# Values' loads on ACT's DMA queue, keys' on SP's: a windowed attention decode step with a gated branch

## Chip, cores and metric

One core of one Trainium2 chip. The metric is the device time of one execution in microseconds; several executions are run and the median is given. The time before is 216.89 us (median of 3 runs, 216.76 to 216.92).

## What is computed

Two tokens (batch 2, one new position each) go through an attention over the last 4096 positions of a cache of 32768, and through a small gated branch; the attention's output is scaled by the branch's. Cut to what matters:

```
W = 4096                                   # window: the last W of Sk = 32768 positions
xn = layernorm(x)                          # x: 2 x 1 x 512
q  = (xn @ wq) as 32 heads of 128          # wq: 512 x 4096
k  = k_cache[:, :, Sk-W:, :]               # 2 x 8 x W x 128, each kv head serves 4 query heads
v  = v_cache[:, :, Sk-W:, :]
p  = softmax(q k^T * 128**-0.5)
s  = (p v, heads joined) @ wo              # wo: 4096 x 512
z  = gelu(xn @ w_in)                       # w_in: 512 x 1792
g  = silu(z1 * (w_sp * layernorm(z2) + b_sp) @ w_out)
out = x + s * g
```

All is float32. The windows of keys and values are 33.6 MB each, wq and wo 8.4 MB each, w_in and w_out 5.5 MB together: every byte is read once and used for one or two vectors.

## The kernel before

The 16 pairs of batch and kv head are taken two at a time: eight *units* (`NU`), each with one tile of keys (`k0` to `k7`) and one of values (`v0` to `v7`). Such a tile is 128 partitions x 32 KB, 4 MB, and is loaded by one DMA (`load`, L146). Keys, values, w_in, wq and wo all share one ring of four buffers of that size (`ring`, L105; `slot`, L111). A load can be issued only when the tile that used its buffer four allocations earlier is no longer read. In order of allocation the ring holds win, wq0, wq2, k0, k1, v0, k2, v1, k3, v2, k4, v3, k5, v4, k6, v5, k7, v6, v7, wo0, wo1. So from k3 on a key tile waits for the key tile two units earlier to have been turned (its last step is T:u.7), and from v2 on a value tile for the value tile two units earlier to have been multiplied (pv:u.1); v7, wo0 and wo1 wait for T:6.7, pv:5.1 and T:7.7.

Every DMA of the bulk is issued by SP, in the order in which the program names it. ACT issues four small loads at the start (x twice, w_sp, b_sp). The order of the steps on every engine is written out by hand in `ORDER` (L27 to L52): a word like `T:3.5` is step T of unit 3, part 5. The words are walked from first to last (L607 to L611), `step` (L572) calls the function, and `InOrder` (L55) makes each engine keep that order. [...]

The steps of a unit, with engine and names in the profile:

- `T` (`turn`, L377, DVE): eight transposes in blocks that turn the keys, `kts<-k`. Two buffers hold half a unit each.
- `shares` (L387, PE, `sh<-kts,qb`), `keep` (L397, ACT, `ss<-sh`), `scores` (L401, PE, `s<-ss,sums`): the scores of one half.
- `rowmax`, `mg`, `shmax`, `bias` (DVE, PE): the maximum and the bias `nb`; `exp` (L430, ACT, `p<-s,nb`); `probs_t` (L438, DVE, `pT<-p`).
- `pv` (L455, PE, `acc<-v,pT`): the values, half a unit each; `lsum`, `shsum`, `weights` (DVE, PE): the sums' reciprocals.
- `evac` (L466, ACT, `o<-acc,wd`), `col`, `gather`, `spread`, `oT`: the unit's output, brought into the layout of the product with wo.
- `X`, `Y`, `U` (`wo_early`, L530, PE, `part<-wo,oT`) and `Z` (`wo_last`, L548, PE, `so<-wo,oT`): the product with wo, block by block as its six DMAs land (`load_wo`, L518).

Steps of two units are interleaved: pv:u.0 stands behind T:(u+1).6 and scores:(u+1).0 behind pv:u.0, so that PE multiplies unit u's values while DVE turns unit u+1's keys. In `ORDER` the words `K:u+1 V:u` stand together at the start of a line, behind evac:u-2 of the line before (V:0 and V:1 behind nothing of that kind), and V:7 stands before wo:0. The hand-written order of unit 2's line, as an example:

```
K:3 V:2 T:2.0 T:2.1 T:2.2 rowmax:1.1 mg:1 shmax:1 T:2.3 bias:1 shares:2.0 T:2.4 exp:1.0 probs_t:1.0 T:2.5 T:2.6 exp:1.1
keep:2.0 pv:1.0 lsum:1 shsum:1 scores:2.0 T:2.7 shares:2.1 probs_t:1.1 pv:1.1 weights:1 keep:2.1 scores:2.1 evac:1
```

In the profile nearly all instructions have line L65, the helper's, so groups are told apart by their tiles.

Of the kernel before, what the change touches and what calls it, by code (L numbers as in the profile page):

```python
# [70 lines left out]
def kernel(  # L71
# [14 lines left out]
    pe, dve, act, sp = (InOrder(tc, e) for e in (nc.tensor, nc.vector, nc.scalar, nc.sync))  # L86
# [24 lines left out]
    def slot(name, *shape):  # L111
        return ring.tile([P, *shape], F32, tag="slot", name=name)
# [14 lines left out]
    for a in range(0, KT, 2):  # L127
        t = slot(f"wq{a}", 2, HQ * DH)
# [14 lines left out]
    NU = NP // 2  # L143
    UJ = 2 * NT

    def load(u, src, name):  # L146
        t = slot(f"{name}{u}", UJ, DH)
        b, v = divmod(u, HKV // 2)
        first = src[b, 2 * v, SK - W, :]
        of = bass.AP(tensor=src.tensor, offset=first.offset, ap=[[UJ * DH, P // 2], [SK * DH, 2], [1, UJ * DH]])  # L150
        sp.dma_start(t.rearrange("p j d -> p (j d)"), of)
        return t


# [120 lines left out]
    u = cst.tile([P, 2, FT, B], F32, tag="u", name="u")  # L275
# [65 lines left out]
    def place_queries():  # L341
        dve.tensor_tensor(
            free_ap(qb, 16, [[REP, G], [32, NP * G], [1, REP]]), free_ap(qa, 0, [[0, G], [REP, NP * G], [1, REP]]),
            free_ap(grpm, 0, [[1, G], [0, NP * G], [0, REP]]), op=ALU.mult,
        )
# [3 lines left out]
    def silu():  # L349
        dve.tensor_scalar(gate, ys, -1.0, 80.0, op0=ALU.mult, op1=ALU.min)  # L350
        act.activation(gate, gate, AF.Exp)
        dve.tensor_scalar_add(gate, gate, 1.0)
        dve.reciprocal(gate, gate)
        dve.tensor_mul(gate, gate, ys)
# [139 lines left out]
    def spread(i):  # L494
        o1, oT, nj = sets[f"oT{i}"]
        pts[i] = bank(f"oT_ps{i}", B, 32)
        pe.matmul(pts[i], perms[nj][0].rearrange("p h a x -> p (h a x)"), o1, start=True, stop=True)

    def place(i):
        _, oT, nj = sets[f"oT{i}"]  # L500
        nx = 32 // nj
        t = sb.tile([P, B, nx, nj], F32, tag="ot", name=f"ot{i}", bufs=1)
        dve.tensor_tensor(
            t, pts[i].rearrange("p b (x j) -> p b x j", x=nx), free_ap(perms[nj][1], 0, [[0, B], [1, nx], [0, nj]]),
            op=ALU.mult,
        )
        dve.tensor_reduce(
            oT[:, :, 0 : 16 * B : 16].rearrange("p j b -> p b j"), t.rearrange("p b x j -> p b j x"), axis=AX.X, op=ALU.add
        )
# [8 lines left out]
    def load_wo(n):  # L518
        t = slot(f"wo{n}", 16, D)
        a = 0  # L520
        for i in ((0,), (1, 2))[n]:
            for j, n in (((0, 16),), ((0, 8),), ((0, 4), (4, 2), (6, 1), (7, 1)))[i]:
                sp.dma_start(t[:, a : a + n, :], wo_s[i][:, j : j + n, :])
                blocks.append((t[:, a : a + n, :], sets[f"oT{i}"][1], j))
                a += n
# [4 lines left out]
    def wo_early(n, at):  # L530
        nonlocal done
        if done == 0:
            part.append(ps.tile([P, 512], F32, tag="s0", name="part"))
        t, oT, j = blocks[n]
        for a in range(at, at + 2):
            g = done % G
            pe.matmul(
                part[0][32 * g : 32 * g + 32, :], oT[:, j + a, :], t[:, a, :], start=(done < G), stop=(done >= EARLY - G)
            )
            done += 1  # L540
# [3 lines left out]
    def copy_parts():  # L544
        parts.append(sb.tile([P, D], F32, tag="o", name="parts", bufs=1))
        act.activation(parts[0], part[0], AF.Copy)

    def wo_last(n):  # L548
        if n == 0:
            so.append(bank("so", DC))  # L550
        t, oT, j = blocks[3 + n]
        for a in range(t.shape[1]):
            for g in range(G):
                pe.matmul(
                    so[0][32 * g : 32 * g + 32, :], oT[:, j + a, :], t[:, a, g * DC : (g + 1) * DC],
                    start=(n == 0 and a == 0), stop=(j + a == oT.shape[1] - 1),
                )

    def add_parts():
        for g in range(G):  # L560
            pe.matmul(
                so[0][32 * g : 32 * g + 32, :], rowm, parts[0][:, g * DC : (g + 1) * DC], start=False, stop=False
            )
# [8 lines left out]
    def step(name, u, a=()):  # L572
        if name == "q":
            place_queries()
        elif name == "silu":
            silu()
        elif name == "K":
            units[u].k = load(u, k_cache, "k")
        elif name == "V":
            units[u].v = load(u, v_cache, "v")  # L580
        elif name == "wo":
            load_wo(u)
        elif name == "spread":
            spread(u)
        elif name == "oT":
            place(u)
        elif name == "X":
            wo_early(0, 2 * a[0])
        elif name == "Y":
            wo_early(1, 2 * a[0])  # L590
        elif name == "U":
            wo_early(2, 2 * a[0])
        elif name == "Z":
            wo_last(u)
        elif name == "parts":
            copy_parts()
        elif name == "pz":
            add_parts()
        else:
            STEPS[name](units[u], *a)  # L600

    units = []
    for u in range(NU):
        p = Unit()
        p.u, p.m, p.kt, p.sh, p.ss, p.s, p.p, p.pT = u, None, {}, {}, {}, {}, {}, {}
        units.append(p)
    for line in ORDER.strip().split("\n"):  # L607
        for name in line.split():
            name, at = name.split(":")
            u, _, a = at.partition(".")  # L610
            step(name, int(u), (int(a),) if a else ())  # L611
# [33 lines left out]
```

## Time and profile before

| | before |
|---|---|
| median of the runs | 216.89 us (216.76 to 216.92) |
| the profiled execution | 217.29 us, span 215.5 us |
| mean granted TensorE clock | 0.825 |
| busy: PE / DVE / ACT / POOL | 143.2 / 126.7 / 51.6 / 4.5 us |
| read from HBM | 89.40 MB, 415 GB/s over the span |
| keys, issue to landing (median of 8) | 27.4 us |
| values, issue to landing (median of 8) | 29.8 us |
| DVE waiting for keys, in total | 29.5 us, 7 times |
| PE waiting for values, in total | 4.3 us, 5 times |

The span runs from the first to the last instruction of the program; the time has some 1.8 us more around it. "Busy" leaves out instructions that only issue a DMA or wait for a semaphore. A DMA queue is named by its number: q1 carries what SP issues, q10 what ACT issues; both are served by the same 16 DMA engines, and q8 and q14 fetch instructions. `SPq` and `ACTq` are the two engines' instruction streams, where a DMA's issue appears with the time that issuing took, not the time of the transfer. Behind "<-" in square brackets stands what ended the idle time before an instruction.

### The profile page before, as it was taken

To read this page: it belongs to the slowest core of one execution; us is meant where nothing else is said; L and a number is where in the kernel's file an instruction comes from. 1 tells how busy PE (TensorE), PEld (TensorE's weight loads), DVE (VectorE), ACT (ScalarE), POOL (GpSimd) and SP (SyncE) were. 2 spreads that over 40 slices of the span, in tenths; PEclk is the share of its full clock that TensorE was granted. 3 is DMA by queue.
4 is the path that set the end of the run, shared out by engine and by line. 5 is a ranking of instruction groups with operands and counts; after the bars stand their busy time and mean duration, and the time that the engine had idled before them with its cause. 6 is when DMAs were issued, how large, how long until landed. Compare 5 with 4: busy or idle time off the path is not lost.

```text
span 215.5 us, 2332 instructions
## 1 busy us (share of the span) xinstructions
PE 143.2 (66%) x900; PEld 48.1 (22%) x900; DVE 126.7 (59%) x218; ACT 51.6 (24%) x129; POOL 4.5 (2%) x17
## 2 busy tenths in 40 slices
PE   0179796833854966964991795389259917987793
PEld 0117622111120221222220231123112201232231
DVE  2611213169899799649928972993698099636011
ACT  5011103300116036033330602142051206142201
POOL 8000000000000000000000000000000000000000
PEclk9999569665998896796697599669755997996999
DMA  7999999999999999999999999999999999999990
GB/s 246 432 443 444 398 429 465 414 458 414 456 408 447 420 426 444 426 443 426 450 420 450 408 441 420 426 450 426 447 415 456 401 456 414 447 426 417 420 374 22
DMA packets 3930, 89.54 MB, mean 416 GB/s; under 512 B 446, under 2 KB 462, under 8 KB 848
## 3 DMA queue, kind: packets, MB, share of 16 engines
q1 hardware_dynamic: 3900, 89.40, 96.8%
q8 instruction: 7, 0.11, 0.2%
q14 instruction: 3, 0.02, 0.0%
q10 hardware_dynamic: 20, 0.01, 0.0%
HBM read 89.40 MB, written 0.00 MB: 415 GB/s over the span
## 4 chain that ended last, share of the span: by engine, by line
DMA 63%; PE 23%; DVE 8%; ACT 3%; issue 1%; ACTq 0%
DMA v<-in_A_v_cache_dram 42%; DMA k<-in_A_k_cache_dram 16%; PE acc L65 10%; DMA win<-in_B_w_in_dram 5%; PE sh L65 5%; DVE kts L65 4%; PE part L65 4%; PE s L65 3%; DVE pT L65 1%; ACT p L65 1%; ACT o L65 1%; DVE gate L65 1%; PE mo L65 1%; ACT ss L65 1%; DVE qb L65 1%
## 5 line engine op out<-in xcount | busy, mean ns | idle before, releaser
L65 DVE STREAM_TRANSPOSE kts<-k 128x1024 f32<-128x1024 f32 x64 | 75.6, 1218 | 29.5 <-DMA k<-in_A_k_cache_dram 29.5
L65 PE MATMUL sh<-kts,qb 128*32 128x512 f32 x256 | 41.6, 775 | 13.2 <-DVE kts L65 9.3
L65 PE MATMUL acc<-v,pT 128*32 128x512 f32 x256 | 37.4, 707 | 8.8 <-DVE pT L65 4.4
L65 ACT ACTIVATE p<-s,nb 128x512 f32<-128x512 f32 x32 | 22.5, 733 | 36.2 <-DVE nb L65 36.2
L65 ACT ACTIVATE ss<-sh 128x512 f32<-128x512 f32 x16 | 9.6, 599 | 59.1 <-PE sh L65 59.1
L65 DVE STREAM_TRANSPOSE pT<-p 128x1024 f32<-128x1024 f32 x16 | 19.6, 1225 | 2.3 <-ACT p L65 2.1
L65 PE MATMUL s<-ss,sums 128*128 128x512 f32 x32 | 18.8, 671 | 2.3 <-ACT ss L65 2.3
L65 PE MATMUL mo<-mg,joint 128*128 128x16 f32 x16 | 4.0, 327 | 23.4 <-DVE mg L65 23.4
L65 PEld LDWEIGHTS acc<-v,pT 128*32 128x32 f32 x256 | 10.5, 145 | 35.1 <-issue 27.0
L65 PEld LDWEIGHTS sh<-kts,qb 128*32 128x32 f32 x256 | 8.8, 126 | 34.2 <-issue 28.8
L65 DVE TENSOR_REDUCE m<-s 128x1 f32<-128x512 f32 x16 | 10.7, 671 | 4.2 <-PE s L65 4.2
L65 PE MATMUL q_ps<-wq,xnT 128*32 128x512 f32 x64 | 10.5, 784 | 3.5 <-DMA wq<-in_A_wq_dram 3.5
L65 ACT ACTIVATE o<-acc,wd 128x128 f32<-128x128 f32 x32 | 9.1, 368 | 15.0 <-PE acc L65 15.0
L65 PEld LDWEIGHTS mo<-mg,joint 128*128 128x128 f32 x16 | 3.2, 250 | 27.2 <-DVE mg L65 24.4
L65 PE MATMUL z<-win,xnT 128*32 128x448 f32 x32 | 5.6, 869 | 4.7 <-DMA win<-in_B_w_in_dram 4.7
L65 PE MATMUL part<-wo,oT 128*32 128x512 f32 x56 | 7.7, 596 | 1.4 <-ACT o L65 1.4
L65 PEld LDWEIGHTS s<-ss,sums 128*128 128x128 f32 x32 | 5.0, 197 | 10.3 <-issue 7.7
L65 PE MATMUL zT_ps<-rowm,z 128*128 128x2 f32 x28 | 6.6, 370 | 0.0
L65 PEld LDWEIGHTS zT_ps<-rowm,z 128*128 128x128 f32 x28 | 6.5, 325 | 0.0
L65 ACT ACTIVATION_READ_ACCUMULATOR p<-s,nb 128x1 f32 x32 | 6.5, 203 | 0.0
L65 ACT ACT_TABLE_LOAD x4 | 5.1, 1283 | 2.6 <-POOL hT L164 2.6
L65 DVE COPY z<-z 128x448 f32<-128x448 f32 x2 | 1.3, 626 | 7.5 <-PE z L65 7.5
(111 smaller groups left out, 68.4 us busy)
## 6 DMA issues: line engine op xcount, KB each, us to landing
k<-in_A_k_cache_dram SPq DMA_DIRECT2D x8, 4096.0 KB, 27.4
v<-in_A_v_cache_dram SPq DMA_DIRECT2D x8, 4096.0 KB, 29.8
wq<-in_A_wq_dram SPq DMA_DIRECT2D x1, 4096.0 KB, 24.5
wq<-in_A_wq_dram SPq DMA_DIRECT2D x2, 2048.0 KB
wo<-in_A_wo_dram SPq DMA_DIRECT2D x1, 4096.0 KB, 30.4
win<-in_B_w_in_dram SPq DMA_DIRECT2D x1, 3584.0 KB, 11.5
wo<-in_A_wo_dram SPq DMA_DIRECT2D x1, 2048.0 KB
wout<-in_B_w_out_dram SPq DMA_DIRECT2D x1, 1792.0 KB, 15.3
```

The costliest lines, as they stand in the source:

```text
L65: return self.tc.keep_in_program_order(call(*args, **kwargs))
```

## The change

`load` is given the engine that issues the DMA. Keys are issued by SP as before, values by ACT, except the last unit's, which SP issues as before. The words of `ORDER`, the ring, the tiles and all computation are the same.

```diff
-    def load(u, src, name):
+    def load(u, src, name, queue):
         t = slot(f"{name}{u}", UJ, DH)
         b, v = divmod(u, HKV // 2)
         first = src[b, 2 * v, SK - W, :]
         of = bass.AP(tensor=src.tensor, offset=first.offset, ap=[[UJ * DH, P // 2], [SK * DH, 2], [1, UJ * DH]])
-        sp.dma_start(t.rearrange("p j d -> p (j d)"), of)
+        queue.dma_start(t.rearrange("p j d -> p (j d)"), of)
         return t
...
         elif name == "K":
-            units[u].k = load(u, k_cache, "k")
+            units[u].k = load(u, k_cache, "k", sp)
         elif name == "V":
-            units[u].v = load(u, v_cache, "v")
+            units[u].v = load(u, v_cache, "v", act if u < NU - 1 else sp)
```

In the built program seven DMA issues leave SP's stream. In ACT's stream v0 stands behind `ys`, v1 behind keep:0.1, and v2 to v6 behind evac:0 to evac:4. The streams of PE, DVE and POOL are the same instruction for instruction.

## The prediction

> **What bounds the kernel now.** I read the page first for the share of the DMA engines, then a table by stretches for where they are full, then the chain that ended last for what the end waits on, then the timelines of the queues and engines that the edit touches.
>
> ```profile
> span 215.5 us, 2332 instructions
> ...
> q1 hardware_dynamic: 3900, 89.40, 96.8%
> ```
>
> The profiled execution took 217.29 us, 1.8 more than its span and 0.4 above the median of the runs (216.89). All 89.40 MB of real loads go through one queue, q1 (SP's), and keep the 16 DMA engines busy for 96.8% of the span. By stretches (PE, PEld, DVE, ACT and POOL busy, then PE clock, DMA share, GB/s):
>
> ```profile
> 52.00:102.00 50.00, 35.32 (x206) 10.20 (x210) 41.02 (x55) 13.15 (x36) 0.00 (x0) 0.84 1.00 429
> ...
> 152.00:202.00 50.00, 33.66 (x200) 10.27 (x200) 32.37 (x51) 14.33 (x40) 0.00 (x0) 0.80 1.00 430
> 202.00:210.00 8.00, 7.49 (x66) 2.86 (x66) 0.78 (x3) 0.01 (x1) 0.00 (x0) 1.00 0.95 395
> ```
>
> The DMA share is 1.00 from 52 to 202 and drops only with the last bytes (0.95 from 202 to 210). So the loads are the floor, no compute engine is (DVE, the busiest, has 41.0 of 50), and a change of queue cannot shorten what is already gapless. It can change the order in which 4 MB transfers land. The end does depend on that order. From the chain in order of time (start, length, what):
>
> ```profile
> 77.09 27.29 DMA v<-in_A_v_cache_dram
> ...
> 150.21 32.33 DMA v<-in_A_v_cache_dram
> ```
>
> These are units 2 and 6: v2 lands at 77.09 + 27.29 = 104.38, v6 at 150.21 + 32.33 = 182.54. Between them land k4 v3 k5 v4 k6 v5 k7 v6, eight transfers in 78.16 us, so one 4 MB transfer takes 9.77 us. Counting back 13 transfers from v6, k1 landed at about 55.5. From v6 on, the end is a chain of computation (PE):
>
> ```profile
> 182.68 1.95 PE L65 MATMUL acc<-v,pT 128*32 128x512 f32 x16 [1.12 <-DMA v<-in_A_v_cache_dram]
> ...
> 185.62 1.97 PE L65 MATMUL sh<-kts,qb 128*32 128x512 f32 x16
> ...
> 198.80 1.95 PE L65 MATMUL acc<-v,pT 128*32 128x512 f32 x16
> 202.11 2.34 PE L65 MATMUL part<-wo,oT 128*32 128x512 f32 x18 [1.36 <-ACT o L65]
> ```
>
> These rows are pv:6.0, shares:7.1, pv:7.1, then the first of the early wo products X. Between pv:7.1's end (200.75) and the first X (202.11) lie 1.36 us. The row names ACT's o, which these matmuls don't read. wo's first transfer is two behind v6, 182.54 + 2 x 9.77 = 202.08, and that is what X waited for. So this tail has two nearly equal gates: the wo loads, which the edit doesn't make later, and the chain from pv:6.0, with 1.36 us of slack.
>
> **The change part by part.** Nothing in work or bytes is removed or added. Seven DMA issues leave SP's instruction stream and stand in ACT's, each where V:u stands in the written order; PE, DVE and POOL keep their instructions.
>
> *SP without them.* Keys were issued when DVE had freed their buffer; no values' issue ahead of them held them up:
>
> ```profile
> 32.50 0.53 SPq L65 DMA_DIRECT2D v<-in_A_v_cache_dram  x1
> 39.53 0.54 SPq L65 DMA_DIRECT2D k<-in_A_k_cache_dram  x1
> 56.46 0.54 SPq L65 DMA_DIRECT2D v<-in_A_v_cache_dram  x1
> 71.88 0.54 SPq L65 DMA_DIRECT2D k<-in_A_k_cache_dram  x1
> 77.09 0.54 SPq L65 DMA_DIRECT2D v<-in_A_v_cache_dram  x1
> ```
>
> Each issue takes 0.54 us and the queue sits for 5 to 17 us between them, so SP saves 7 x 0.54 us that nobody waited for: nothing gained.
>
> *ACT with them.* The neighbours in ACT's order:
>
> ```profile
> 46.04 0.28 ACT L65 ACTIVATE ys<-y_sum 128x128 f32<-128x128 f32 x1 [3.37 <-PE y_sum L65]
> 55.34 0.60 ACT L65 ACTIVATE ss<-sh 128x512 f32<-128x512 f32 x1 [9.01 <-PE sh L65]
> 59.24 0.60 ACT L65 ACTIVATE ss<-sh 128x512 f32<-128x512 f32 x1 [3.31 <-PE sh L65]
> 63.39 0.31 ACT L65 ACTIVATE gate<-gate 128x128 f32<-128x128 f32 x1 [3.55 <-DVE gate L65]
> ...
> 77.09 1.14 ACT L65 ACTIVATE o<-acc,wd 128x128 f32<-128x128 f32 x4 [1.06 <-PE acc L65]
> 81.21 0.74 ACT L65 ACTIVATE p<-s,nb 128x512 f32<-128x512 f32 x1 [2.98 <-DVE nb L65]
> ```
>
> v0 follows ys, v1 the second ss (keep:0.1), and v2 to v6 the o of evac:0 to evac:4. The buffer of each is already free there (evac:u needs the same pv:u.1 that frees v:u), so ACT does not wait at the issue; 0.54 us falls into idle times of 9.01, 3.55 and 2.98; exp of the later units waits for nb in the same way. Cost on ACT: none, covered by that wait; with that cover gone it would be 0.54 us per unit ahead of exp. The issues come later, though: v1 at 59.84 instead of 56.46, v2 at 78.23 instead of 77.09 (evac's 1.14). Those two stand behind some 28 us of queue and cost nothing. v0 moves most, from 32.50 to 46.32, and that puts k2 (39.53) ahead of it in time.
>
> *Two queues instead of one.* This is the term that counts. The trace has one stretch in which ACT's queue (q10) holds packets while SP's has win, wout and wq outstanding. ACT's small loads are issued at
>
> ```profile
> 0.74 0.55 ACTq L65 DMA_DIRECT2D xs<-in_A_x_dram  x1
> 1.33 0.24 ACTq L65 DMA_DIRECT2D wb<-in_B_w_sp_dram  x1
> 1.59 0.27 ACTq L65 DMA_DIRECT2D wb<-in_B_b_sp_dram  x1
> 1.90 0.63 ACTq L65 DMA_DIRECT2D x<-in_A_x_dram  x1
> ```
>
> and the DMA queues show, from 2 to 5.8 us (first row) and from 5.8 to 11.4 (the two after it), packets, MB and share:
>
> ```profile
> q1 hardware_dynamic: 39, 1.12, 70.6%
> ...
> q1 hardware_dynamic: 103, 2.37, 98.0%
> q10 hardware_dynamic: 16, 0.00, 0.3%
> ```
>
> After xs, no packet of q10 passes for four microseconds from the last issue (1.90 to 5.8); then 16 pass while q1 is 98.0% busy. q1's bytes of the two stretches, 3.49 MB, are fewer than win's 3.67 (128 x 7168 floats), so those 16 passed inside the first bulk load, with wout and wq queued behind it. So a second queue is neither put behind all of the first's bytes nor served at once: it waits for some packets already taken in, and then both are served in turns. For 32 KB packets on both sides I take turns as half the rate each.
>
> [...]
>
> Let s be the time of v0's first packet. After s, seven values' transfers go at half rate beside keys, so v6 lands 14 transfer times later: s + 14 x 9.77 = s + 136.8. Lower bound of s: xs, on empty queues, was issued at 0.74 and read by DVE at 2.15,
>
> ```profile
> 2.15 0.68 DVE L65 BATCH_NORM_STATS2 st<-xs 2x6 f32<-2x512 f32 x1
> ```
>
> 1.4 us, so 46.32 + 1.4 = 47.7. Upper: behind all that was queued on SP, k1's end, 55.5 (q10's last packets waited 9.5 us: 55.8). I take a wait of 5 us, nearest to the first q10 packets (5.8 minus 1.33 is 4.5, and the packets are a little larger here): s = 51.3. Then v6 lands at 188.1, 5.6 late. pv:6.0 moves by that, everything behind it on PE too, and the 1.36 of slack ahead of X is used up first: **+4.2 us**.
>
> The keys pay for what the values gain. k1 has 55.5 - s left at s and needs twice that; k2 to k7 follow at 2 x 9.77 each; so k7 lands 55.5 - s late (4.2 at s = 51.3). DVE then turns it:
>
> ```profile
> 172.91 1.25 DVE L65 STREAM_TRANSPOSE kts<-k 128x1024 f32<-128x1024 f32 x1 [6.66 <-DMA k<-in_A_k_cache_dram]
> ...
> 181.86 2.33 DVE L65 STREAM_TRANSPOSE kts<-k 128x1024 f32<-128x1024 f32 x2
> ```
>
> The last turn ended at 184.19 and shares:7.1 began at 185.62: 1.43 of slack. So shares:7.1 is late by 54.1 - s through k7 and by s - 45.7 through v6, whichever is more. The least of the two together is 4.2 (s = 49.9), which leaves +2.8 at the end: no s makes it free. At s = 47.7 it is 6.4 through k7, +5.0. At s = 55.5 it would be 9.8 through v6, +8.4; but k3 is issued at 71.88, only some 3 us before k2 lands (55.5 + 2 x 9.77 = 75.0), so with such waits SP's queue runs dry at each unit and the values catch up; I cap this end at +6.5. Everything after X keeps its lengths. wo0's issue waits for pv:5.1 and slips by as much, but v7 is in flight ahead of it until 182.54 + 9.77 = 192.3, so wo lands as before. In the middle the same lateness makes PE wait for v in each unit and shows nowhere at the end.
>
> Sum: SP 0, ACT 0, landing order +4.2 (+2.8 to +6.5). 217.29 + 4.2 = 221.5 for a profiled execution, 216.89 + 4.2 = **221.1 us** for the median.
>
> **The rivals.** *No slower: turns by whole transfers.* With k1 in service at 46.3, ACT's v0 would go next (landing 65), then k2, v1, k3, the order of now, and v6 lands at 182.5: 216.9. For it: a bulk load on both queues is nowhere in the trace. Against: the 16 packets inside win's 10 us. [...] 8%.
>
> *Values first.* If ACT's queue is favoured, v6 changes places with k7, which lands at about 182.5, 9.6 late; less 1.43 and 1.36 that is +6.8: 223.7. Against: q10's own packets were spread over 5.6 us. 10%.
>
> *The values catch up.* SP runs dry often and s is small, so that v6 is only 3 late: +1.5, 218.4. Against: the sum of both latenesses above. 5%.
>
> *Faster.* Two queues would have to move bytes quicker. q1's 96.8% leaves 6.9 us, nearly all of it the start and the 5.5 us after the last load, so at most 0.5: 216.4. 3%.
>
> **How the numbers follow.** The forecast has 74%, the rivals 8, 10, 5 and 3. 218.4 to 224.0 holds the forecast with its bounds, the catching-up case and values first, and leaves out 8 + 3 and some of the tails. Slower by over 0.2% (0.43 us, about what the runs can tell) 0.89, within it 0.08, faster 0.03.
>
> **What would show it.** The last wo transfers still land near 212 and the DMA share stays 1.00 to 202, with about 7 x 4.19 = 29.4 MB on q10. v6 lands near 188 and k7 near 177 (before: 182.5, 172.7). PE's wait for v before pv rises to several microseconds per unit. The first X starts near 206 and is released by PE's own pv:7.1, not by a load. wo0 is issued near 177. If landings of k and v alternate at 9.7 us as now, turns are by transfer and I am wrong; if the DMA share falls inside the span, a queue ran dry on both sides and the sum is too small.

## The result, and the profile after

| | before | after |
|---|---|---|
| median of the runs | 216.88 us (216.76 to 216.92, 4 runs) | 219.24 us (218.37, 218.41, 220.07, 220.12) |
| ratio to before | | 1.0111 (95% interval 1.0085 to 1.0136) |
| the profiled execution | 217.29 us, span 215.5 | 218.37 us, span 216.6 |

The change makes the kernel 2.4 us slower. The four runs stand in two pairs 1.7 us apart, and a second set of the same kernel (first experiment) is slower still, 221.18 us, outside the interval of the first: an interval covers the scatter within its set, not the difference between sets. The profile below belongs to the lower pair.

The queues first, in the page of the changed kernel (packets, MB, share of 16 engines):

```profile
span 216.6 us, 2328 instructions
...
q1 hardware_dynamic: 2892, 60.04, 64.7%
q10 hardware_dynamic: 1028, 29.37, 31.5%
```

29.37 MB have moved to q10; the two shares together, 96.2%, are what q1 had alone (96.8). By stretches of the changed kernel (PE, PEld, DVE, ACT, POOL busy, PE clock, DMA share, GB/s):

```profile
52.00:102.00 50.00, 36.05 (x196) 10.49 (x196) 35.24 (x47) 11.84 (x31) 0.00 (x0) 0.77 1.00 430
...
152.00:202.00 50.00, 34.14 (x226) 10.89 (x224) 33.06 (x51) 14.92 (x41) 0.00 (x0) 0.86 1.00 430
202.00:210.00 8.00, 7.61 (x76) 3.06 (x76) 1.68 (x8) 1.14 (x4) 0.00 (x0) 1.00 0.95 392
```

DMA share and GB/s are those of before: the transfers run at full rate with no gap and end at the same time, within 0.7 us. Only their order is different. The DMA queues of the changed kernel from 120 to 180 us:

```profile
q10 hardware_dynamic: 443, 12.94, 50.1%
q1 hardware_dynamic: 443, 12.94, 50.0%
```

Packet for packet, half and half. The start of this sharing, from 46 to 50 and from 50 to 54 us (a packet is 32 KB):

```profile
q1 hardware_dynamic: 49, 1.57, 91.8%
...
q10 hardware_dynamic: 31, 1.02, 58.8%
q1 hardware_dynamic: 21, 0.69, 39.8%
```

v0 is issued at 46.50 and its queue moves nothing until 50; its first packet is at 50.25. Then the keys. The first transpose of k7, which stood at 172.91 before (DVE, changed kernel):

```profile
178.42 1.25 DVE L65 STREAM_TRANSPOSE kts<-k 128x1024 f32<-128x1024 f32 x1 [6.00 <-DMA k<-in_A_k_cache_dram]
```

k7 is 5.5 us late. v6 is late as well, but by less: the last of its 128 packets ended at 185.1, against 181.3 before. The tail on PE, changed kernel:

```profile
183.87 3.64 PE L65 MATMUL sh<-kts,qb 128*32 128x512 f32 x16
187.50 2.12 PE L65 MATMUL acc<-v,pT 128*32 128x512 f32 x16
189.56 1.12 PE L65 MATMUL s<-ss,sums 128*128 128x512 f32 x2
190.62 1.97 PE L65 MATMUL sh<-kts,qb 128*32 128x512 f32 x16
...
200.28 1.95 PE L65 MATMUL acc<-v,pT 128*32 128x512 f32 x16 [1.38 <-DVE pT L65]
...
202.48 1.95 PE L65 MATMUL acc<-v,pT 128*32 128x512 f32 x16
204.25 2.32 PE L65 MATMUL part<-wo,oT 128*32 128x512 f32 x18
...
208.00 3.64 PE L65 MATMUL part<-wo,oT 128*32 128x512 f32 x32
```

pv:6.0 (187.50) no longer waits for v6; it follows shares:7.0 (183.87) without a gap, and that needed k7. In the kernel before, shares:7.0 was done 1.12 us ahead of pv:6.0, which then waited for v6:

```profile
178.36 3.20 PE L65 MATMUL sh<-kts,qb 128*32 128x512 f32 x16 [0.32 <-DVE nb L65]
```

So all of k7's 5.5 reaches shares:7.0, which also takes 0.4 longer; less the 1.12 that makes pv:6.0 4.8 late. Against before, shares:7.1 is 5.0 late, pv:7.1 3.7, the first X 2.1, and the span 1.1. So 3.7 us of lateness disappear between pv:6.0 and the end, and the rows say where. In the kernel before, pv:7.0 and the last products with wo (X, at 202.11, stands in the prediction):

```profile
195.29 3.27 PE L65 MATMUL acc<-v,pT 128*32 128x512 f32 x16 [1.38 <-DVE pT L65]
...
205.87 4.71 PE L65 MATMUL part<-wo,oT 128*32 128x512 f32 x32
```

pv:7.0 took 3.27 and takes 1.95 now (1.3); X waited 1.36 and waits no more; the last 32 products with wo took 4.71, because they waited for wo's second transfer as well (its last packet ended at 206.41), and take 3.64 now (1.1). The wait stands behind the first four of the 32, in the chain that ended last (kernel before):

```profile
205.94 0.98 PE part L65 x4
206.93 0.03 issue
206.95 3.64 PE part L65 x28
```

That the 1.36 were a wait for wo, which the profile of before put down to ACT, is named in the profile of a kernel with the same tail (small loads on ACT, below):

```profile
201.77 2.34 PE L65 MATMUL part<-wo,oT 128*32 128x512 f32 x18 [0.88 <-DMA wo<-in_A_wo_dram]
```

### The profile page after: what moved, and what is told of

Read it like the earlier page. It is cut to its first block, busy times and chain, and to the rows that moved or that the text cites. A ratio compares the mean times of both kernels' runs of the same rounds, so it can differ in the third digit from the quotient of the medians.

```text
span 216.6 us, 2328 instructions
## 1 busy us (share of the span) xinstructions
PE 142.5 (66%) x900; PEld 50.1 (23%) x900; DVE 126.5 (58%) x218; ACT 51.8 (24%) x129; POOL 4.5 (2%) x17
## 3 DMA queue, kind: packets, MB, share of 16 engines
q10 hardware_dynamic: 1028, 29.37, 31.5%
## 4 chain that ended last, share of the span: by engine, by line
DMA 62%; DVE 18%; PE 14%; ACT 4%; issue 1%; ACTq 0%; DVEq 0%
DMA k<-in_A_k_cache_dram 56%; DVE kts L65 13%; DMA win<-in_B_w_in_dram 5%; PE acc L65 4%; PE part L65 3%; ACT p L65 3%; PE z L65 3%; PE sh L65 3%; DVE pT L65 2%; DVE m L65 1%; PE s L65 1%; DVE gate L65 1%; ACT o L65 1%; DVE nb L65 0%; PE mo L65 0%
## 5 line engine op out<-in xcount | busy, mean ns | idle before, releaser
L65 PE MATMUL sh<-kts,qb 128*32 128x512 f32 x256 | 46.1, 848 | 12.4 <-DVE kts L65 9.3
L65 PE MATMUL acc<-v,pT 128*32 128x512 f32 x256 | 33.6, 637 | 2.8 <-DVE pT L65 2.8
L65 PE MATMUL mo<-mg,joint 128*128 128x16 f32 x16 | 4.6, 369 | 32.6 <-DVE mg L65 32.6
L65 PEld LDWEIGHTS acc<-v,pT 128*32 128x32 f32 x256 | 11.7, 143 | 25.7 <-issue 14.1
L65 PEld LDWEIGHTS sh<-kts,qb 128*32 128x32 f32 x256 | 9.3, 135 | 36.2 <-issue 32.7
L65 PE MATMUL q_ps<-wq,xnT 128*32 128x512 f32 x64 | 11.0, 819 | 3.7 <-DMA wq<-in_A_wq_dram 3.7
L65 PEld LDWEIGHTS mo<-mg,joint 128*128 128x128 f32 x16 | 3.8, 295 | 36.4 <-DVE mg L65 32.2
L65 PE MATMUL part<-wo,oT 128*32 128x512 f32 x56 | 6.6, 594 | 0.0
```

What stands on the lines that cost most here:

```text
L65: return self.tc.keep_in_program_order(call(*args, **kwargs))
```

## The experiments

The theory, called landing order below: two queues are served in turns, the transfers are as fast as ever, and the price is what the last keys or values (k7, v6) land late. Its rivals: ACT's stream pays (0.54 us per issue, later issues, v0's above all), or a second queue costs by itself. Each kernel was timed in turns with the kernel before, on the same chip. "k7" here and in the table is the start of its first transpose.

**The changed kernel again.**

> The changed kernel again. Theory (landing order): the whole price is that k7 lands at about 178.4 instead of 172.7 because keys and values share the DMA engines in turns; ratio about 1.011, with single times at two levels, near 218.4 and near 220.1, as in the four runs so far. If the higher level comes from the phase of the turns, a profile at that level shows k7 some 1.7 us later, or pv:7.0 at its slower length (3.27 instead of 1.95 us) with k7 landing as before. Rival (ACT's stream: the issues and their later times cost): the same total, nothing told apart here.

Measured: 221.11 to 221.59 (4 runs), ratio 1.0204 (1.0191 to 1.0217); a third level, not the two of the first set. Its profile has a span of 219.4, 2.8 more than the first. DVE's timeline of it:

```profile
179.84 1.25 DVE L65 STREAM_TRANSPOSE kts<-k 128x1024 f32<-128x1024 f32 x1 [5.80 <-DMA k<-in_A_k_cache_dram]
```

That is k7's first transpose on DVE. In the same profile pv:6.0, pv:7.0 and pv:7.1 on PE:

```profile
188.92 1.95 PE L65 MATMUL acc<-v,pT 128*32 128x512 f32 x16
...
201.59 2.76 PE L65 MATMUL acc<-v,pT 128*32 128x512 f32 x16 [1.38 <-DVE pT L65]
...
204.80 2.50 PE L65 MATMUL acc<-v,pT 128*32 128x512 f32 x16
```

k7 is 1.4 later and pv:6.0 with it; pv:7.0 and pv:7.1 take 5.26 instead of 3.90, another 1.4. Both guesses of the expectation hold, each with half; the ratio that it gave, 1.011, does not. This set ran on chip 1, and the first set's chip is not on record, so a difference between chips is not ruled out; the kernel before took 216.85 there, and 216.83 to 217.04 in the other sets. In the stretch of pv:7.0 the granted clock was 0.69 here, 1.00 in the first profile and 0.58 in the kernel before.

**All but v6 on ACT.**

```diff
-            units[u].v = load(u, v_cache, "v", act if u < NU - 1 else sp)
+            units[u].v = load(u, v_cache, "v", act if u < NU - 2 else sp)
```

> Values of units 0 to 5 on ACT's queue, v6 and v7 on SP's behind k7. Landing order: by then ACT's queue has run empty before k7 is served, so k7 lands at 172 to 174 and v6 at 182.5 as in the kernel before: 216.9 to 217.5, although six of the seven moved issues are still on ACT. Rival (ACT's stream): six sevenths of the price stays, about 218.9. Rival (two queues make transfers slower): about 218.9 too, and the DMA share or the bytes per second fall in the middle.

Measured: 218.09 median, 216.80 to 219.72 (10 runs), ratio 1.0054 (1.0030 to 1.0078). Half a miss: k7 is on time, and the profiled execution ends with a span of 215.2 like before, but the runs scatter and their middle lies between the expectation (up to 217.5) and the rivals (218.9), so the time alone does not decide. The PE rows of this kernel (shares:6.0, scores:6.0, pv:5.0, pv:6.0) show what was still late:

```profile
163.78 3.64 PE L65 MATMUL sh<-kts,qb 128*32 128x512 f32 x16 [3.45 <-DVE kts L65]
...
168.19 2.08 PE L65 MATMUL s<-ss,sums 128*128 128x512 f32 x2 [0.25 <-ACT ss L65]
170.20 3.21 PE L65 MATMUL acc<-v,pT 128*32 128x512 f32 x16
...
185.91 2.18 PE L65 MATMUL acc<-v,pT 128*32 128x512 f32 x16 [0.70 <-DVE pT L65]
```

In the kernel before shares:6.0 and pv:5.0 stood at:

```profile
158.66 3.64 PE L65 MATMUL sh<-kts,qb 128*32 128x512 f32 x16 [3.23 <-DVE kts L65]
...
165.07 3.02 PE L65 MATMUL acc<-v,pT 128*32 128x512 f32 x16
```

Both are 5.1 late: k6, for which shares:6.0 waits, still shared its way with values (v4 and v5 were issued by ACT at 119.75 and 137.44), and PE's order carries 3.2 of it to pv:6.0 (182.68 before), which waits for no load now. The expectation of the run with v5, v6 and v7 on SP, below, "v5 some 5 us late", names the wrong load: v5 was late too, but pv:5.0 does not wait for it.

**Only v6 on ACT.**

```diff
-            units[u].v = load(u, v_cache, "v", act if u < NU - 1 else sp)
+            units[u].v = load(u, v_cache, "v", act if u == NU - 2 else sp)
```

> Only v6 on ACT's queue. Landing order: v6, issued near 151, passes half of what SP has queued (rest of v5, k7), lands near 175 and k7 only near 182, 9.6 late; less 1.4 ahead of shares:7.1 and some 4 of slack ahead of the wo products (5.0 of lateness became 1.1 in the profile of the changed kernel): +4 to +5.5, 221 to 222.4, more than with all seven moved. Rival (ACT's stream): one seventh of the price, 217.2. Rival (slower transfers): one seventh, 217.2.

Measured: 223.44 (222.47 to 223.69, 5 runs), ratio 1.0286 (1.0264 to 1.0307). One load moved costs more than seven, a little more than expected, and both rivals are out by 6 us. DVE's row has the reason:

```profile
182.12 1.25 DVE L65 STREAM_TRANSPOSE kts<-k 128x1024 f32<-128x1024 f32 x1 [15.86 <-DMA k<-in_A_k_cache_dram]
```

v6 is issued at 150.33, 4.9 us after k7 (145.46), and k7 pays for nearly a whole transfer: 182.12 - 172.91 = 9.2 late. By the theory v6 is served beside the transfers that still stand in SP's queue, and k7 is behind them.

**Small loads on ACT.** The values stay on SP; ACT spends the issues alone. `tiny` is read by nothing.

```diff
             units[u].v = load(u, v_cache, "v")
+            if u < NU - 1:
+                act.dma_start(tiny, x[:, 0, :P])
```

> All values on SP as before; ACT instead issues seven small loads of x (2 x 128 floats, into a tile that nothing reads) at the seven places where the change has it issue values. Landing order: 216.9, within 0.2%. Rival (ACT's stream): most of the price, 218 to 219, as ACT spends the same 0.54 us at the same seven places.

Measured: 216.94 (216.81 to 217.31, 11 runs), ratio 1.0006 (0.9997 to 1.0014). The issues on ACT cost nothing. They were shorter than meant, 0.24 us each in the trace and not the 0.54 of a 4 MB load, so this run tests 1.7 us of issuing where the change adds 3.8. Full issues on ACT, five of them, are in the run with v5, v6 and v7 on SP, below.

**The order alone, on one queue.** The kernel before with two words exchanged.

```diff
-K:7 V:6 T:6.0 rowmax:5.1
+V:6 K:7 T:6.0 rowmax:5.1
```

> The kernel before, all loads on SP's queue, with one pair of words in the order exchanged: V:6 ahead of K:7. No second queue. Landing order: v6 lands near 172.7 and k7 near 182.5; from the first transpose of k7 to the end of the span it took 38.2 us in the changed kernel, 39.6 in its second profile and 39.6 with only v6 on ACT, so the span is 220.7 to 222.1 and the time 222.5 to 223.9, the same as with only v6 on ACT. Rival (a second queue costs by itself): 216.9, since there is only one.

Measured: 223.15 (222.61 to 225.15, 4 runs), ratio 1.0307 (1.0267 to 1.0348), k7 at 182.13. With one queue and k7 landing just as late (182.12 with only v6 on ACT) the price of "only v6 on ACT" is there again, within its interval. Within what this run can tell (0.4%), a second queue costs nothing by itself here; the order in which the last two loads land is the whole price.

**v5, v6 and v7 on SP, v0 to v4 on ACT.**

```diff
-            units[u].v = load(u, v_cache, "v", act if u < NU - 1 else sp)
+            units[u].v = load(u, v_cache, "v", act if u < NU - 3 else sp)
```

> Values of units 0 to 4 on ACT's queue, v5, v6 and v7 on SP's. With v6 alone on SP, k7 landed in time (first transpose at 172.64) but v5 some 5 us late, and PE's order carried that to the end. Landing order: here v5 lands at 162.7 and k7 at 172.5 as in the kernel before, five loads still go by ACT, and the time is 216.7 to 217.2 with no run above 217.5. Rival (a second queue costs by itself): five sevenths of the price, 218.5 to 220.

Measured: 216.86 (216.79 to 217.32, 11 runs), ratio 1.0002 (0.9994 to 1.0011). Five of the seven loads go by ACT, with issues of 0.54 to 0.60 us and v0 issued as late as in the changed kernel (46.48), and nothing is lost at the end. From 147 on, 68 us ahead of the end, q10 moves no more data and the queue is one again: the last packets of k6, v5 and k7 end at 152.0, 162.0 and 171.6, as before (152.2, 161.9, 171.6). pv:6.0 is still 1.2 late (183.90), which the slack worked out below covers. So neither ACT's issues nor v0's late one set the price.

**v0 back on SP.**

```diff
-            units[u].v = load(u, v_cache, "v", act if u < NU - 1 else sp)
+            units[u].v = load(u, v_cache, "v", act if 0 < u < NU - 1 else sp)
```

> v0 back on SP, v1 to v6 on ACT. v0 is the load whose issue the change delays most (13.8 us). Landing order: v0 now stands ahead of k2 on SP, the keys come later still at first (k2 near 86 instead of 77), ACT's queue runs dry once or twice and they get half of it back; k7 lands near 180 and v6 near 188: 220.5 to 223, no better than with all seven. Rival (v0's late issue is what costs): 217.

Measured: 222.01 (220.82 to 222.25, 5 runs), ratio 1.0218 (1.0195 to 1.0241), k7 at 180.83. Undoing the part that looked worst, v0's late issue, does not help.

**All eight values on ACT.**

```diff
-            units[u].v = load(u, v_cache, "v", act if u < NU - 1 else sp)
+            units[u].v = load(u, v_cache, "v", act)
```

> All eight values on ACT, v7 too. Landing order: v7 goes in turns with wo's first transfer and lands near 204 instead of 192; pv:7.0 begins near 204.5 instead of 200.3, and 13.2 us later (as from pv:7.0 to the last PE instruction in the changed kernel, 200.3 to 213.3) PE is done: span about 220.5 to 222, time 222 to 224. Rival (ACT's stream): one eighth more than the changed kernel, 219.5.

Measured: 221.63 (221.21 to 221.92, 4 runs), ratio 1.0219 (1.0205 to 1.0233), a little under the expectation. v7 is now the late one, but by less than a full turn:

```profile
201.56 3.18 PE L65 MATMUL acc<-v,pT 128*32 128x512 f32 x16 [1.83 <-DMA v<-in_A_v_cache_dram]
```

The second set of the changed kernel had the same ratio (1.0204), so this run does not tell what v7 costs.

**v0's issue pinned.** The time at which ACT issues v0 differs between executions: it went out 0.06 to 0.07 us after the start of `ys`, behind which it stands, at 44.40 to 47.79 in five profiles. A copy that waits for DVE was put ahead of it.

```diff
         elif name == "V":
+            if u == 0:
+                act.activation(tiny, qb[:, 0:4], AF.Copy)
...
-K:0 K:1 V:0 T:0.0 q:0 T:0.1
+K:0 K:1 T:0.0 q:0 V:0 T:0.1
```

> The changed kernel with one small copy more on ACT, of four columns of qb, right ahead of v0's issue, so that v0 is issued when DVE has written qb, near 48.6, instead of at a time that varied from 44.4 to 47.8 between profiles. In two profiles of the changed kernel an issue at 46.50 went with the first transpose of k7 at 178.42, one at 44.70 with 179.84: nearly one for one. Landing order: k7's first transpose at 176 to 177, v6 lands near 187, the span 215.5 to 217.5, the time 217.3 to 219.3 in all runs. Rival (the levels are noise of the TensorE clock): the same levels from 218.4 to 221.6 as the changed kernel.

Measured: 221.00 (220.00 to 222.24, 6 runs), ratio 1.0175 (1.0147 to 1.0203). The kernel missed its aim: columns 0 to 3 of qb are not written by `q`, nothing was waited for and v0 went out at 44.59. It is one more sample of the changed kernel, with k7 at 180.78. Mended:

```diff
-                act.activation(tiny, qb[:, 0:4], AF.Copy)
+                act.activation(tiny, qb[:, 16:20], AF.Copy)
```

> As the pinned kernel before, but the copy ahead of v0's issue reads columns 16 to 19 of qb, which DVE does write (columns 0 to 3, read before, are not written by that step, and v0 went out at 44.59 without waiting; k7's first transpose was at 180.78 there). Now v0 is issued at 48.5 to 49. Landing order: one for one with the four profiles (issue 46.50, 44.70, 44.59, 44.40; first transpose of k7 178.42, 179.84, 180.78, 179.33), k7 comes at 175.5 to 177; v6 then lands near 187 and is about as late; span 215.5 to 217.5, time 217.3 to 219.3, and the runs lie within 1.5 us of each other. Rival (the levels are noise of the TensorE clock, or of which packet goes first): 219 to 222 with the same scatter.

Measured: 222.27 (221.72 to 224.19, 6 runs), ratio 1.0266 (1.0232 to 1.0301). v0's issue at 49.08, right after the copy (49.00), which had waited 2.31 us for DVE; k7 at 177.01: at the edge of what was expected. The time is not: it lies above the expectation and just above the rival's 219 to 222, and the runs scatter by 2.5 us, not 1.5. The values are now the later ones, and PE runs slowly behind the wait (granted clock 0.54):

```profile
188.18 3.58 PE L65 MATMUL acc<-v,pT 128*32 128x512 f32 x16 [2.58 <-DMA v<-in_A_v_cache_dram]
```

**v0 later still.**

```diff
-K:0 K:1 V:0 T:0.0 q:0 T:0.1 T:0.2 T:0.3 shares:0.0 T:0.4 T:0.5 T:0.6 keep:0.0 scores:0.0 T:0.7
+K:0 K:1 T:0.0 q:0 T:0.1 T:0.2 T:0.3 shares:0.0 T:0.4 T:0.5 T:0.6 keep:0.0 V:0 scores:0.0 T:0.7
```

> The changed kernel with V:0 moved in the order behind keep:0.0, so that ACT issues v0 near 56, nearly 10 later. Landing order: k1 lands undisturbed at 55.5 and k2 early, v0 near 75 to 79 and pv:0.0 waits for it; then SP's queue runs dry while DVE waits behind PE, ACT's catches up, and the two end as close together as before: k7 between 173 and 178, v6 between 186 and 192, whichever is later sets the end; 218 to 222, so even 10 us more on v0 do not add 10. Rival (v0's late issue is what costs): some 5 to 10 us on top of the changed kernel, 224 and more.

Measured: 221.48 (219.29 to 222.56, 6 runs), ratio 1.0193 (1.0151 to 1.0235): no more than the changed kernel although v0 is issued 10 us later, at 56.55. The profiled execution has k7 at 178.03 and pv:6.0 waiting for v6:

```profile
188.48 1.95 PE L65 MATMUL acc<-v,pT 128*32 128x512 f32 x16 [1.86 <-DMA v<-in_A_v_cache_dram]
```

**All profiles in one table.** "Slow" is what pv:6.0, pv:7.0 and pv:7.1 took over 1.95 us each. The fifth column is pv:6.0's start + 29.0 + slow; the 29.0 is taken from "v0 later", which has no slow.

| kernel | k7 | pv:6.0 | slow | + 29.0 | span |
|---|---|---|---|---|---|
| before | 172.91 | 182.68 | 1.3 | 213.0 | 215.5 |
| small loads on ACT | 172.66 | 182.44 | 1.6 | 213.0 | 215.3 |
| v5, v6, v7 on SP | 172.53 | 183.90 | 1.4 | 214.3 | 215.1 |
| v6, v7 on SP | 172.64 | 185.91 | 0.2 | 215.2 | 215.2 |
| changed | 178.42 | 187.50 | 0.2 | 216.7 | 216.6 |
| changed, again | 179.84 | 188.92 | 1.4 | 219.3 | 219.4 |
| copy of columns 0 to 3 | 180.78 | 189.86 | 1.5 | 220.4 | 220.4 |
| v0 pinned | 177.01 | 188.18 | 3.0 | 220.2 | 220.2 |
| v0 later | 178.03 | 188.48 | 0.0 | 217.5 | 217.5 |
| v0 on SP | 180.83 | 189.92 | 1.4 | 220.3 | 220.4 |
| all eight on ACT | 179.33 | 188.42 | 1.4 | 218.8 | 219.4 |
| only v6 on ACT | 182.12 | 191.20 | 1.5 | 221.7 | 221.7 |
| order alone | 182.13 | 191.22 | 0.8 | 221.0 | 221.0 |

From pv:6.0 on the end is fixed to 0.1 us, unless the last loads end it, at 215.1 to 215.5, or pv:7.0 waits for v7 (all eight on ACT, 0.6 more). The kernel before had 2.5 us of slack there (215.5 - 213.0); the two waits for wo, 1.36 and 1.1, add up to the same.

## Why the prediction was right, and where not

*The floor.* Right: DMA share 1.00 to 202, the same GB/s, the same end of the loads.

*ACT and SP.* Right in the price: seven short issues at the same places cost 0.06%, inside their interval, and five full ones 0.02%. The times of the issues were not: the prediction put v2's behind evac's 1.14, but it goes out as the first `o` begins (last section).

*Turns.* Right: 443 packets each. v0's first packet came at 50.25; the sum had taken 51.3, a wait of 5 us where 3.75 was measured. That the wait is for packets already taken in was the author's estimate; the traces show only how long it was. The queues change within one transfer: from 50 to 54, less than half of one transfer's 9.77 us, they moved 1.02 and 0.69 MB, and k7 was late, which turns by whole transfers would have left where it was.

*Landing order.* Right in kind. k7 was forecast 4.2 late and is 5.5 (6.9 in the second profile); v6 was forecast 5.6 late, and its last packet is 3.9 late. The wait of v0 is the term that moved both: with 50.25 for s the prediction's own sums give 5.25 for k7 and 4.5 for v6. v6 was to hold pv:6.0 itself; pv:6.0 came 4.8 late, but behind the keys, and the changed kernel's list of waits has none for values at all. The prediction had followed k7 to shares:7.1 alone, with 1.43 of slack, and left out the way through shares:7.0, which stands ahead of pv:6.0 and had 1.12. The forecast that PE would wait several microseconds for values in each unit failed with it; of the kernels with v0 to v6 on ACT, such waits came in the two with v0 issued later still (21.0 us in total with v0 pinned, 18.5 with v0 later). That keys and values pay for each other is what these two kernels showed, and none of the issue times of v0 that were run, by SP or by ACT at 44.40 to 56.55, makes the change free.

*The end.* Here is the step that was mis-sized: "the 1.36 of slack ahead of X is used up first". The slack was 2.5 us, as the products with wo behind X waited for wo's second transfer too, and in this execution pv:7.0 ran at a granted clock of 1.00, 1.3 less than in the profile of before (0.58). So of 4.8 us 1.1 were left in the profiled execution, and +2.4 in the median of that set, little over half of the +4.2 that was forecast. The second set's 221.18 meets the forecast's 221.1 by luck: in its profile pv:6.0 was 6.2 late where 5.6 was forecast, the slack was 2.5 where 1.36 was, and PE was as slow as before.

*Rivals.* Whole transfers by turns: out. Faster: out, the time rose. Values first: not what the changed kernel did, with k7 5.5 late and not 9.6; its landing order was made on purpose twice (only v6 on ACT, order alone) and cost 6.3 to 6.6 us, forecast +6.8. The values catch up: its 218.4 is the profiled execution's time by chance, for the queues moved equal shares from 120 to 180, v6 was 3.9 late, and the lateness that counted was the keys'.

## What to carry to other kernels

Where one queue already filled the DMA engines, as here (430 GB/s with one queue and with two), the second queue added no bandwidth; it took half of it (443 packets of 886 from 120 to 180) away from the queue whose data were needed first. Ask of each load which transfers it will now be served beside, and which of those is awaited last: here one load moved near the end cost 2.9%, five moved ahead of it nothing. Slack at an end is found by following all its gates, not the first one only.

## What was not expected of the hardware

An issue on ACT did not wait for the activations ahead of it to finish. In the changed kernel v2's stands behind four `o` in the program, and went out while the first ran (ACT, the four, split by the issue):

```profile
80.30 0.37 ACT L65 ACTIVATE o<-acc,wd 128x128 f32<-128x128 f32 x1 [1.06 <-PE acc L65]
80.37 0.54 ACTq L65 DMA_DIRECT2D v<-in_A_v_cache_dram  x1
80.57 0.87 ACT L65 ACTIVATE o<-acc,wd 128x128 f32<-128x128 f32 x3
```

The same 16 matmuls of pv:7.0, after the same wait of 1.38 to 1.39 us, took 1.95 us in some executions and up to 3.5 in others, with a granted clock of 1.00 and of 0.53 to 0.58; lengths and clocks in between occur too (2.76 at 0.69). What decides was not settled. Together pv:6.0, pv:7.0 and pv:7.1 were up to 3 us slower for it, which reaches the end once the loads no longer set it.

Kernels with a late tail scatter by 0.5 to 3.3 us between runs, while the kernel before, which ends with its loads, stayed within 216.56 to 217.50 in its 62 timed runs. The clock is a likely reason, and the time of v0's issue may be another; neither is shown, as each kernel was profiled once and only the changed one twice. Behind `ys` the issue fell between 44.40 and 47.79 in the profiles. In the four of them in which v0 to v6 go by ACT and nothing holds v0 back, k7 was at 178.42 (issue 46.50), 179.84 (44.70), 180.78 (44.59) and 179.33 (44.40): the earliest issue did not bring the latest k7.
